# Attention and a Fourier mixing layer on one core: the mixing's chunk sums formed in two instalments, and the second weight matrix's combinations spread over 22 products instead of 28

## The chip, the cores and the metric

The kernel runs on one core of a Trainium2 chip. The metric is the device time of one execution in microseconds (us). A core has a matrix engine (PE, TensorE, with its weight loads shown apart as PEld), a vector engine (DVE, VectorE), a scalar engine (ACT, ScalarE), a general engine (POOL, GpSimd) and a queue that issues nearly all transfers (SP). [...]

## The reference

There are 8 batches. For each batch, 8 heads of attention with 576 positions and a head width of 64 give a matrix `x` of 576 by 512. A score counts only if it lies within `tau` of its row's maximum. Then `x` goes through a two-dimensional Fourier transform, whose real part is added to it, through a normalization and through two matrices with a ReLU between them:

```
scores = scale * q @ k.T;  thresh = max(scores) - tau
attn = softmax(where(scores >= thresh, scores, -1e9));  x = attn @ v      # 8 heads side by side: 576 x 512
X = fft(fft(x, axis=1), axis=2);  u = x + real(X)
un = (u - mean(u)) / sqrt(var(u) + 1e-6)
out = u + relu(un @ w_ch1) @ w_ch2          # w_ch1: 512 x 2048, w_ch2: 2048 x 512
```

## The kernel before, in words

**Attention steps.** Heads are handled in pairs, four pairs a batch, in the order 1, 3, 0, 2 of the four 128-wide chunks of `x` (`PAIRS`). A pair takes five steps of 128 query rows (the fifth takes the last 64 rows of both heads), so a batch is 20 steps and the whole is 160. A step `i` is called here by its place in its batch, `i % 20`. A step computes scores on PE (L440, L446), row maxima on DVE (L520), exponentials on ACT (L526), the threshold on DVE (L540), the division on ACT (L549); one step later PE transposes the weights through PSUM (L587, L605) and ACT copies them out (L593, L607). Every second step or so PE multiplies with `v` (L636).

**Mixing.** The Fourier transform uses the symmetries of sine and cosine. When a pair of heads is done, `fold_rows` adds and subtracts mirrored rows of its chunk of `x` and writes the chunk `f[:, p, :]`: an even half `E` of 304 columns and an odd half `O` of 304 columns. The first three pairs are folded by POOL (L687, L692, L699, L703), the last one by DVE, in step 1 of the next batch. After that the four chunks are combined with each other, which is what the change touches. With c0 to c3 for the chunks:

- `fold_halves`, on POOL, when chunks 1 and 3 are there: c1+c3 goes to the tile `sums`, c1-c3 replaces c3 (L718, L719, 608 columns each).
- `mixing`, on DVE, when the last chunk (2) is there: c0+c2 and c0-c2 (L718, L719, 608 columns each), then five sums and scaled sums of 304 columns (L744, L740 three times, L749). They stand in three pieces: two 608-column operations; `f0E` and `f1E`; then `f2E`, `f3O` and `f0O`.

PE then multiplies the results with cosine and sine tables (L759): first `py` of the even halves, which reads f0E, f1E and f2E in this order, later `py` of the odd halves, which reads f0O and f3O. ACT copies each `py` out of PSUM (L764, L769). PSUM tiles of this kind, also those of the transposes and of the matrix products, share four buffers (tag `mm`).

The pieces of `mixing` are handed out by `mix(1)`. In the main loop (batches 2 to 7) the first piece stands on DVE behind the thresholds of step 2 (L540). The second comes later in the same step, after PE has transposed the first half of the weights of step 1. The third comes in step 3, behind that step's maxima on DVE (L520) and its exponentials on ACT (L526). The `py` products of PE stand after it.

**The two matrices.** The tokens of all batches form groups of 512 (`NG` = 9). Group 0 is computed plainly (`channels`); the others use a two-level scheme with seven products instead of eight at each level (`two_level`), in which combinations of weight blocks stand in place of the blocks. The combinations of both matrices are formed once, written to DRAM (`f1`, `f2`) and then read back for each group in transfers of 1 MB to three buffers in turn (L1067, `ensure`). `w2_forms` is the generator that forms those of the second matrix on DVE and POOL (L1002) and sends them to DRAM from SP (L1012, L1016, L1019, and L1028 for the combinations, which stand in `room`, the tile `w1[3]`). Its last 16 pieces are taken in `two_level` of group 1, at chosen ones of the seven products of each of the four parts (L1236). When all products of the first matrix are through, POOL forms `s1_tile` in four operations (L1149). `s1_tile` is the same memory as `room`. After it POOL forms combinations of the hidden layer (L1184) that PE needs for the second matrix's products (L1391).

**What sets the order.** Everything from L104 on stands in an order written by hand (`manual_schedule`). A budget in `fill` decides how many of the two matrices' products are put into each step: it counts matrix columns, not time. `fold_more` takes one piece of a pair's folding per call; it is called in steps with `t > 2` and from `background`.

## Time and profile before

| | |
|---|---|
| time, median of three executions | 1574.54 us (1570.67 to 1574.88) |
| time of the profiled execution | 1571.28 us |
| its span, first to last instruction | 1569.5 us |
| PE busy | 1530.0 us, 97% |
| DVE busy | 1059.4 us, 68% |
| ACT busy | 917.8 us, 58% |
| POOL busy | 774.2 us, 49% |
| mean share of the TensorE clock granted | 0.993 |

A group of the profile is one line of the kernel on one engine with its count, its busy time, the mean length of one, and the idle time of the engine just before such instructions with the instruction that ended it ("10.6 <-DVE f L740 8.8": 10.6 us idle in all, 8.8 of it ended by DVE at L740). In a timeline, the first column is the start, the second the length, and a bracket at the end is the idle time before it and its releaser. The matrix engine records two entries for each fp32 product. The records of PE are modelled at their ends, so a gap between two of them is the least that it stood still.

### The profile page before, as it was taken

The page shows a single profiled execution, that of the slowest core. Times are in us where ns is not written, and L with a number is a line of the kernel's source. Part 1 is how long each engine was busy: PE and PEld are TensorE (multiplying, and loading weights), DVE is VectorE, ACT ScalarE, POOL GpSimd, SP SyncE. Part 2 cuts the span into 40 slices and gives each one's busy share as a digit, 9 for nine tenths or more (in the row PEclk, how much of TensorE's full clock was granted, in tenths as well). Part 3 has the DMA queues.
Part 4 walks back from the last instruction along what each step waited for, and adds up shares of the span by engine and source line. Part 5 has one row for each costly group of instructions (what it writes and reads, how often), then busy time and mean ns, then how long its engine had stood idle before and what let it go on. Part 6 is the DMA issues. An engine that isn't in the chain of part 4 may idle for free.

```text
span 1569.5 us, 27006 instructions
## 1 busy us (share of the span) xinstructions
PE 1530.0 (97%) x9786; PEld 1190.0 (76%) x9786; DVE 1059.4 (68%) x2119; ACT 917.8 (58%) x1921; POOL 774.2 (49%) x962
## 2 busy tenths in 40 slices
PE   9999999999989999999999999999999999999999
PEld 4555555556778778877788878887787878889999
DVE  6987676746769466766577566856677666755546
ACT  6875675655646576656666666666666676232231
POOL 3774553034355643546254724554264625546735
PEclk9999999999999999999999999999999999999999
DMA  6423234366756354634464354635464434646655
GB/s 167 129 58 117 77 91 116 125 204 178 240 185 197 86 175 130 180 108 144 144 184 138 116 148 140 194 94 159 128 189 132 143 118 148 222 143 234 234 201 182
DMA packets 248907, 239.31 MB, mean 152 GB/s; under 512 B 197027, under 2 KB 218533, under 8 KB 228678
## 3 DMA queue, kind: packets, MB, share of 16 engines
q1 hardware_dynamic: 246262, 237.28, 49.3%
q8 instruction: 78, 1.28, 0.3%
q10 hardware_dynamic: 2512, 0.30, 0.1%
q14 instruction: 55, 0.45, 0.1%
HBM read 205.93 MB, written 31.46 MB: 151 GB/s over the span
## 4 chain that ended last, share of the span: by engine, by line
PE 83%; DVE 10%; ACT 3%; DMA 1%; POOL 1%; issue 1%; SPq 0%; DVEq 0%; ACTq 0%; POOLq 0%
PE ph L1203 24%; PE po L1391 17%; PE pv L636 9%; PE sc L440 9%; PE pw L605 7%; PE po L926 4%; PE ph L902 3%; PE sc L446 2%; PE py L759 2%; PE pe L587 1%; PE pa L776 1%; DVE neg L520 1%; PE pa L780 1%; PE po L1370 1%; PE pn L851 1%
## 5 line engine op out<-in xcount | busy, mean ns | idle before, releaser
L520 DVE TENSOR_REDUCE neg<-sc 128x1 f32<-128x576 f32 x216 | 154.2, 751 | 131.2 <-PE sc L440 113.8
L526 ACT ACTIVATE e<-sc,neg 128x576 f32<-128x576 f32 x216 | 158.6, 734 | 120.5 <-DVE neg L520 120.5
L1391 PE MATMUL po<-w,w_all 128*128 128x128 f32 x1728 | 222.2, 278 | 5.1 <-DMA w<-f 2.7
L1391 PEld LDWEIGHTS po<-w,w_all 128*128 128x128 f32 x1728 | 207.6, 194 | 14.6 <-issue 9.1
L1140 DVE TENSOR_TENSOR hs<-ph,hs 128x512 f32<-128x512 f32 (+1 forms) x128 | 105.3, 823 | 164.7 <-PE ph L1203 96.2
L1149 POOL TENSOR_TENSOR w<-hs 128x512 f32<-128x512 f32 x32 | 41.9, 1314 | 310.5 <-ACT hs L1145 231.7
L1203 PE MATMUL ph<-u_t,w 128*128 128x256 f32 x768 | 180.9, 382 | 0.5 <-DMA w<-f 0.5
L540 DVE SCALAR_TENSOR_TENSOR e<-sc,thr,e 128x576 f32<-128x576 f32 x216 | 168.3, 812 | 18.8 <-ACT thr L530 18.7
L607 ACT COPY e_t<-pw 128x512 f32<-128x512 f32 x256 | 148.5, 595 | 54.0 <-PE pw L605 52.5
L605 PE MATMUL pw<-ident,e 128*128 128x128 f32 x1152 | 170.4, 275 | 4.6 <-ACT ends L593 1.9
L440 PE MATMUL sc<-kT,qT 64*128 64x288 f32 x1024 | 167.3, 428 | 6.4 <-DVE e L477 5.8
L549 ACT ACTIVATE e<-e,den 128x576 f32<-128x576 f32 x216 | 157.4, 775 | 8.0 <-DVE den L388 7.3
L1203 PEld LDWEIGHTS ph<-u_t,w 128*128 128x128 f32 x768 | 140.9, 190 | 23.6 <-issue 5.3
L1203 PE MATMUL ph<-w_all,w 128*128 128x256 f32 x672 | 157.1, 382 | 1.1 <-DVE w_all L1125 1.0
L605 PEld LDWEIGHTS pw<-ident,e 128*128 128x128 f32 x1152 | 136.3, 142 | 20.5 <-issue 5.8
L1203 PEld LDWEIGHTS ph<-w_all,w 128*128 128x128 f32 x672 | 123.5, 190 | 23.9 <-issue 4.9
L1145 ACT ACTIVATE hs<-hs 128x512 f32<-128x512 f32 (+1 forms) x96 | 74.1, 772 | 114.0 <-DVE hs L1140 113.4
L440 PEld LDWEIGHTS sc<-kT,qT 64*128 64x128 f32 x1024 | 95.0, 186 | 55.5 <-issue 25.1
L1256 POOL TENSOR_TENSOR w_all<-w_all 128x128 f32<-128x128 f32 (+2 forms) x160 | 116.6, 745 | 30.2 <-DVE w_all L1411 22.4
L1391 PE MATMUL po<-w,hs 128*128 128x128 f32 x912 | 120.0, 278 | 0.0
L1391 PEld LDWEIGHTS po<-w,hs 128*128 128x128 f32 x912 | 109.9, 192 | 9.5 <-issue 8.0
L593 ACT COPY ends<-pe 128x128 f32<-128x128 f32 (+1 forms) x128 | 38.1, 297 | 61.8 <-PE pe L587 41.6
(224 smaller groups left out, 2940.3 us busy)
## 6 DMA issues: line engine op xcount, KB each, us to landing
w<-f SPq DMA_DIRECT2D x150, 1024.0 KB, 4.9
hs<-in_moe_w_ch_dram SPq DMA_DIRECT2D x23, 512.0 KB, 4.7
q_in<-in_q_dram SPq DMA_DIRECT2D x128, 72.0 KB, 4.2
out_dram<-u SPq DMA_DIRECT2D x36, 256.0 KB, 2.3
k_in<-in_k_dram SPq DMA_DIRECT2D x124, 72.0 KB, 2.4
v_in<-in_v_dram SPq DMA_DIRECT2D x64, 128.0 KB, 5.1
f<-w SPq DMA_DIRECT2D x14, 512.0 KB, 3.3
f<-w SPq DMA_DIRECT2D x7, 1024.0 KB, 4.8
```

Of the source, the lines that this page charges most:

```text
L440: nc.tensor.matmul(sc[j][:, c, 0:HALF], qT[hp, 128 * t : 128 * t + 128], kT[hp, k0 + HALF * c : k0 + HALF * (c + 1)], start=True, stop=True,)
L520: nc.vector.tensor_reduce(out=neg[:, j : j + 1], in_=sc[j][:, :, 0:HALF], axis=AXIS_XY, op=ALU.max, negate=True,)
L526: nc.scalar.activation(out=ej, in_=sc[j][:, :, 0:HALF], func=ACT.Exp, bias=neg[:, j : j + 1], scale=1.0)
L540: nc.vector.scalar_tensor_tensor(out=ej, in0=sc[j][:, :, 0:HALF], scalar=thr[:, j : j + 1], in1=ej, op0=ALU.is_ge, op1=ALU.mult, accum_out ...
L549: nc.scalar.activation(out=e[:, S * j : S * (j + 1)], in_=e[:, S * j : S * (j + 1)], func=ACT.Copy, scale=den[:, j : j + 1],)
L605: nc.tensor.transpose(pw[:, c, :], e[:, c0 : c0 + 128], ident[:, :])
L607: nc.scalar.copy(e_t[:, 4 * j : 4 * j + 4, qs], pw[:, :, :])
L636: nc.tensor.matmul(pv[64 * j : 64 * j + 64, 0:m], vt[:, 2 * c + j, :], e_t[:, 4 * j + c, 0:m] if c < 4 else ends[:, 0, 0:m], start=(c == 0 ...
L1140: nc.vector.tensor_tensor(out=to, in0=bank, in1=to if other is None else other, op=ALU.add)
L1203: nc.tensor.matmul(bank[:, 256 * q : 256 * q + 256].rearrange("p (two n) -> p two n", two=2), left[:, 256 * c + 128 * q : 256 * c + 128 * ...
L1256: return lambda: eng.tensor_tensor(out=to, in0=to, in1=other, op=ALU.add)
L1391: nc.tensor.matmul(to, lefts[m][j][:, s], right_[:, 128 * s : 128 * (s + 1)], start=jn in (0, 4) and s == 0, stop=s == 3, skip_group_check ...
```

## The change

The sums of the chunks are taken apart. What needs chunks 0, 1 and 3 alone is formed ahead, by a new function `partial_sums`, while the last pair of heads is still in attention; when the last chunk is there, five operations of 304 columns are left. The partial results are c0+c1+c3 (E), c0-(c1+c3) (O), a scaled c1+c3 plus c0 (E), and two scaled combinations of c1-c3 with c0 (E and O). In `mixing`, the first piece is then f0E, f1E and f2E, the second f0O, the third f3O.

Batch by batch: in batch 0 the first two partial sums are on POOL and the other three on DVE behind the maxima; in batch 1 all five are on DVE at the end of step 19; in batches 2 to 7 three are on DVE in step 19 and two in step 0 of the next batch. So that chunk 0 is folded by then, `fold_more` is called in step 17 as well. In the diff, the loop over `partial_sums(1)` is batch 1's. The last hunks are in the main loop: there the first `next(partials)` of step 19 stands behind the thresholds of that step, as does that of step 0; the second one of step 19 stands after the transposes of the first half of the weights, ahead of `fill`. One more `next(partials)` behind the loop serves the last batch.

The second part is one number: pieces of `w2_forms` are taken at five of the seven products of a part instead of four, so the sixteenth piece is taken at the 22nd product instead of the 28th.

```diff
     def fold_halves(b):
         sums[b] = sb.tile([128, 2, 2 * FW], FP32, tag="tmp", bufs=1, name="sums")
-        fold_chunks(nc.gpsimd, b, 1)
-
-    def fold_chunks(eng, b, c):
-        eng.tensor_tensor(out=sums[b][:, c, :], in0=f[:, c, :], in1=f[:, c + 2, :], op=ALU.add)
-        eng.tensor_tensor(
-            out=f[:, c + 2, :], in0=f[:, c, :], in1=f[:, c + 2, :], op=ALU.subtract
+        for out_, op in ((sums[b][:, 1, :], ALU.add), (f[:, 3, :], ALU.subtract)):
+            nc.gpsimd.tensor_tensor(out=out_, in0=f[:, 1, :], in1=f[:, 3, :], op=op)
+
+    E, O = slice(0, FW), slice(FW, 2 * FW)
+
+    def scaled(out_, in0, factor, in1):
+        nc.vector.scalar_tensor_tensor(
+            out=out_, in0=in0, scalar=factor, in1=in1, op0=ALU.mult, op1=ALU.add
         )
+
+    def partial_sums(b, eng=nc.vector):
+        s = sums[b]
+        eng.tensor_tensor(out=s[:, 0, E], in0=f[:, 0, E], in1=s[:, 1, E], op=ALU.add)
+        eng.tensor_tensor(out=s[:, 0, O], in0=f[:, 0, O], in1=s[:, 1, O], op=ALU.subtract)
+        yield
+        scaled(s[:, 1, E], s[:, 1, E], flip, f[:, 0, E])
+        yield
+        scaled(f[:, 3, E], f[:, 3, E], minus, f[:, 0, E])
+        scaled(f[:, 3, O], f[:, 0, O], plus, f[:, 3, O])
+        yield
...
-        fold_chunks(nc.vector, b, 0)
+        s = sums.pop(b)
+        for c in range(2):
+            nc.vector.tensor_tensor(out=f[:, c, E], in0=s[:, c, E], in1=f[:, 2, E], op=ALU.add)
+        nc.vector.tensor_tensor(out=f[:, 2, E], in0=f[:, 3, E], in1=f[:, 2, E], op=ALU.subtract)
         yield 0
-        s01 = sums.pop(b)
...
-        nc.vector.tensor_tensor(out=f[:, 0, E], in0=s01[:, 0, E], in1=s01[:, 1, E], op=ALU.add)
-        fold(f[:, 1, E], s01[:, 1, E], flip, s01[:, 0, E])
+        nc.vector.tensor_tensor(out=f[:, 0, O], in0=s[:, 0, O], in1=f[:, 2, O], op=ALU.add)
         yield 0
-        fold(f[:, 2, E], f[:, 3, E], minus, f[:, 2, E])
-        fold(f[:, 3, O], f[:, 2, O], plus, f[:, 3, O])
-        nc.vector.tensor_tensor(out=f[:, 0, O], in0=s01[:, 0, O], in1=s01[:, 1, O], op=ALU.subtract)
+        scaled(f[:, 3, O], f[:, 2, O], minus, f[:, 3, O])
         yield 0
...
-                if at in (0, 2, 4, 6):
+                if at in (0, 2, 3, 4, 6):
                     next(forms, None)
...
+        if first == 19:
+            for _ in partial_sums(1):
+                pass
...
+        if i % per_batch == 19:
+            partials = partial_sums(i // per_batch)
+            next(partials)
+        if i % per_batch == 0 and i > 2 * per_batch:
+            next(partials)
...
-        if t > 2:
+        if t > 2 or i % per_batch == 17:
             fold_more()
+        if i % per_batch == 19:
+            next(partials)
```

The order of instructions on PE and on ACT is the same in both programs. DVE has 18 rows of instructions more, POOL two (the first batch's two partial sums), and SP the same number in another order.

More of the change, by code (lines that the diff above doesn't have):

```diff
@@ L730, in mixing @@
         slot = slice(S * (b % 2), S * (b % 2) + S)
-        E, O = slice(0, FW), slice(FW, 2 * FW)
-        fold_chunks(nc.vector, b, 0)
+        s = sums.pop(b)
+        for c in range(2):
+            nc.vector.tensor_tensor(out=f[:, c, E], in0=s[:, c, E], in1=f[:, 2, E], op=ALU.add)
+        nc.vector.tensor_tensor(out=f[:, 2, E], in0=f[:, 3, E], in1=f[:, 2, E], op=ALU.subtract)
         yield 0
-        s01 = sums.pop(b)
-        def fold(out_, in0, factor, in1):
-            nc.vector.scalar_tensor_tensor(
-                out=out_, in0=in0, scalar=factor, in1=in1, op0=ALU.mult, op1=ALU.add
-            )
-        nc.vector.tensor_tensor(out=f[:, 0, E], in0=s01[:, 0, E], in1=s01[:, 1, E], op=ALU.add)
-        fold(f[:, 1, E], s01[:, 1, E], flip, s01[:, 0, E])
+        nc.vector.tensor_tensor(out=f[:, 0, O], in0=s[:, 0, O], in1=f[:, 2, O], op=ALU.add)
         yield 0
-        fold(f[:, 2, E], f[:, 3, E], minus, f[:, 2, E])
-        fold(f[:, 3, O], f[:, 2, O], plus, f[:, 3, O])
-        nc.vector.tensor_tensor(out=f[:, 0, O], in0=s01[:, 0, O], in1=s01[:, 1, O], op=ALU.subtract)
+        scaled(f[:, 3, O], f[:, 2, O], minus, f[:, 3, O])
         yield 0
@@ L1656, in second_batch @@
             scores(i)
+        partials = iter(())
         if first == 0:
+            partials = partial_sums(0, nc.gpsimd)
+            next(partials)
             transposed_weights(i - 1)
         def behind_maxima():
+            for _ in partials:
+                pass
             if first == 2:
@@ L1720, in second_batch @@
             fold_halves(1)
+        if first == 19:
+            for _ in partial_sums(1):
+                pass
         if first < 3:
@@ L1772 @@
         next(weights, None)
-        if t > 2:
+        if t > 2 or i % per_batch == 17:
             fold_more()
+        if i % per_batch == 19:
+            next(partials)
         fill()
@@ L1798 @@
         held.pop(0)()
+    next(partials)
     weights = weights_in_parts(total - 1)
```

## The prediction

> **What bounds the kernel now.** I read the page's busy shares and its chain first.

> ```profile
> PE 1530.0 (97%) x9786; PEld 1190.0 (76%) x9786; DVE 1059.4 (68%) x2119; ACT 917.8 (58%) x1921; POOL 774.2 (49%) x962
> ...
> PE 83%; DVE 10%; ACT 3%; DMA 1%; POOL 1%; issue 1%; SPq 0%; DVEq 0%; ACTq 0%; POOLq 0%
> ```

> PE sets the end. The change takes no product from PE, so it can win only PE's idle time, 35.8 us by my sum of the gaps between its records, and what products lose at half clock. The groups by line on PE show the gaps that it can touch:

> ```profile
> L1391 PE MATMUL po<-w,w_all 128*128 128x128 f32 x1728 | 222.2, 278 | 5.1 <-DMA w<-f 2.7 <-POOL w_all L1184 2.1 <-ACT ends L593 0.3
> ...
> L759 PE MATMUL py<-dim_c,f 128*128 128x65 f32 (+3 forms) x144 | 21.6, 280 | 10.6 <-DVE f L740 8.8 <-DVE w_all L1411 1.6
> ```

> The second line is the mixing, once a batch; the first one's 2.7 and 2.1 are two single waits in group 1. PE's timeline in batch 5, and then in group 1:

> ```profile
> 1018.32 0.56 PE L759 MATMUL py<-dim_c,f 128*128 128x65 f32 x4
> 1020.90 0.49 PE L759 MATMUL py<-dim_c,f 128*128 128x128 f32 x2 [2.02 <-DVE f L740]
> 1021.22 0.27 PE L587 MATMUL pe<-ident,e 128*128 128x128 f32 x1
> 1021.33 0.60 PE L605 MATMUL pw<-ident,e 128*128 128x128 f32 x4
> 1022.11 0.71 PE L759 MATMUL py<-dim_s,f 128*128 128x128 f32 x4 [0.18 <-ACT y_e L769]
> ```
> ```profile
> 449.55 0.60 PE L605 MATMUL pw<-ident,e 128*128 128x128 f32 x4
> 452.85 1.92 PE L1391 MATMUL po<-w,w_all 128*128 128x128 f32 x8 [2.70 <-DMA w<-f]
> ```

> In batch 5 two `py` products (f0E, f1E) run, and the third waits 2.02 us for f2E, which DVE forms only behind two maxima (1018.22 to 1019.63). The gaps of batches 2 to 7 at this place are 1.18, 1.51+0.70, 2.03, 2.02, 2.03 and 1.56; batch 0 has 0.47, batch 1 none. For group 1, POOL's and SP's timelines say what was late:

> ```profile
> 443.41 1.66 POOL L1002 TENSOR_TENSOR w<-w_all,w 128x512 f32<-128x512 f32 x1 [9.07 <-DVE w L1002]
> 450.27 5.38 POOL L1149 TENSOR_TENSOR w<-hs 128x512 f32<-128x512 f32 x4 [5.20 <-DMA f<-w]
> ```
> ```profile
> 445.10 0.33 SPq L1028 DMA_DIRECT2D f<-w  x1
> 445.52 1.32 SPq L1067 DMA_DIRECT2D w<-f  x2
> ```

> The last combination is formed at 443.41 to 445.07. L1028, which writes it out, blocks SP until 445.10; only then are the loads behind it issued, of which PE waits for one until 452.85. L1149, which overwrites `room`, waits until L1028 has landed, so L1184 ends late and PE waits again, 2.15 us at 456.92. Windows (stretch, length, busy us and count of PE, PEld, DVE, ACT, POOL, then granted clock, DMA share, GB/s):

> ```profile
> 452.90:459.70 6.80, 4.65 (x21) 4.36 (x22) 1.49 (x3) 0.00 (x0) 6.80 (x9) 0.51 0.83 287
> 848.90:852.30 3.40, 3.40 (x15) 3.01 (x15) 3.33 (x10) 1.96 (x5) 0.00 (x0) 0.51 0.41 164
> 1021.00:1024.40 3.40, 3.22 (x26) 2.63 (x27) 3.33 (x10) 2.52 (x7) 0.00 (x0) 1.00 0.41 164
> ```

> So the gaps of group 1, batch 4 and (at 1193.7) batch 6 are followed by half clock, that of batch 5 is not.

> [...]

> **The change part by part.**

> *Second matrix's combinations.* The sixteenth piece comes six products earlier. Group 1's 28 products fill 351 to 441 us, 3.2 each, so L1028 leaves at about 445.1-19 = 426. SP is then free when the loads' buffers are, about 430 at the latest estimate, for products at 449.55: 20 us against a landing of 7.2 us here (median 4.9). L1149 can then start at its relu, about 443.4, and end, at 1.31 each, just after 444.7 for the last; L1184 by about 446, ahead of 451.5, where PE would want it. Gone: 2.70+2.15, and the half clock: 21 records at a spacing of 0.213 instead of 0.111 lose 2.1. **-6.95.** Price: 16.3 us of DVE's work falls into 71 instead of 90 us, 23% for 18%, where DVE is 69% busy and PE already waits 1.85 in all on L1140's release of banks: **+0.5**, from 0 to +3.

> *Mixing, batches 2 to 7.* f2E is now in the first piece, three 304-column operations (1.42-1.47) in place of two of 608 (1.56), so the third `py` product follows the second. What is late next is ACT: the odd `py` needs the bank that ACT's y_e copies free, and these stand behind the exponentials (until 1020.62 in batch 5): 0.63+ later PE goes at about 1021.2 rather than 1022.11. So batch 5 gains 0.9 of 2.0. Likewise batch 2: 0.8; batch 3: 0.36; batch 4: 1.33, with 0.81 of half clock (3.46 instead of batch 5's 2.65 us from the odd `py` to the next scores); batch 6: 0.94+1.56 (4.21 instead of 2.65); batch 7: 1.56, since its wait was on L1411. **-8.3.** If the ACT copies hide as well, all 11.0 of gaps go. Batch 0, its f2E earlier: **-0.5.**

> *DVE's five partial sums.* Per batch DVE had 2x0.78+3x0.526+2x0.47 = 4.1 us; after it has 4.9: two of 0.474 and three of 0.526 ahead, four of 0.474 and one of 0.526 in `mixing`. What matters is that 1.5 us now stands in step 19 and 1.05 in step 0. Behind them on DVE are the maxima of steps 0 and 1, for which ACT's exponentials wait, and then PE's transposes. DVE is idle 0.9 and 0.6 us ahead of those maxima, and the transposes of step 1 stand 1.9 to 2.8 us behind ACT's division. Without POOL the shift is taken up. A POOL operation at the same time adds about 1.0 (1.43 less 0.47) to each: The trace of before can't show how often that happens here; I take one meeting that shows on PE, in one batch of the six: **+1.0**, from 0 to R2's value below. Batch 1 has all five in step 19, 2.5 us, against 2.6 of slack ahead of the scores and 4.0 ahead of the transposes: **+0.2**. With this cover gone each batch would pay its 2.5 us.

> *Moves.* Step 17's extra `fold_more` puts POOL's folds ahead of one or two L1184. Chunk 0 was folded at 799.90 in batch 4, and DVE wants it about 812.6: 12 us to spare, so **0**. Batch 0's two sums on POOL, an estimated 0.8 us each (its 608-column operations take 1.47), stand behind copies of tables where nothing of PE waits for POOL: 0. PE's and ACT's orders don't change. SP has the same transfers.

> Sum: -6.95+0.5-8.3-0.5+1.0+0.2 = **-14.05**. Profiled execution: 1571.28-14.05 = 1557.2. The median of the three lay 3.26 above it: forecast **1560.5 us**.

> **Rivals.**
> R1, half of it: either group 1's wait stays, because its loads run at 0.83 DMA share and land late whenever they go, or `py` waits for its bank and not for f2E, so that the mixing's change doesn't do what it says. For: the 7.2 us landing; ACT's 0.18 in batch 5. Against: the releasers are named DVE f L740 and L1028. Without group 1's part 1574.5-8.8+1.7 = 1567.4; without the mixing's 1574.5-6.95+1.7 = 1569.3. So **1568**.
> R2, slower: DVE's queue at the batch boundary. If all five partial sums meet POOL they take 2.5+5x1.0 = 7.5 us; less 1.5 of idle (0.9+0.6) the exponentials come 6.0 later, against 2.8 of slack: PE waits 3.2 us in six batches, 19.2, and each such wait can bring a half-clock window (half of 3.4: 1.7 us), 10.2. Against gains of 15.75 (6.95+8.3+0.5) that is +13.65: **1588**. Without the windows it decides where the shift passes 2.8+15.75/6 = 5.4 us. For: DVE's forms vary threefold, POOL folds chunk 0 about then. Against: the fold ends 12 us earlier and POOL is 49% busy.
> R3, all of it: full gaps 11.0, batch 0's 0.5, group 1's 4.85, half clock 2.1+2.4, and an estimated 1.6 as the small waits behind them go too, no penalty: -22: **1552**.
> R4, the denser combinations cost their +3: 1563, on the forecast's side.

> **How the numbers follow.** Forecast with R4: 0.60, own range 1555 to 1565; R1 0.20; R3 0.11; R2 0.09. What this measurement can tell from no change is about 0.3%, 4.7 us: 1569.8. Faster holds the forecast, R3, and 0.14 of R1: 0.85; within: 0.06 of R1 and 0.03 of R2's mild end: 0.09; slower 0.06. The 80% range leaves out half of R3 and most of R2 and a little of R1: **1552 to 1570**.

> **What would show it.** Right: L1391 loses its 2.7 and 2.1 and 453 to 460 is at full clock; L1028 issues near 426 and L1149's wait names ACT; L759's idle falls from 10.6 to about 4 and names ACT y_e. Wrong: L587 and L605 gain idle time behind DVE in steps 0 and 1 (R2); L759 keeps its sum under another name (R1); L1140 on DVE delays L1203 (R4); or half-clock windows come back at other gaps, which is what I can least exclude.

## The result and the profile after

The changed kernel takes 1551.36 us in the median of four executions (1549.43 to 1552.64), the kernel before beside it 1573.1 (1570.67 to 1574.88): a ratio of 0.9862, 95% interval 0.9841 to 0.9882. A second set of runs gave 1551.38 us and a ratio of 0.9858 (0.9843 to 0.9874). The forecast was 1560.5; the time lies 9.1 us below it and 0.6 us below the lower end of the 80% range. The direction was right, the size was not.

The profiled executions compare as 1571.28 before (span 1569.5) and 1552.55 after (span 1550.8). The page after, its busy shares and its chain:

```profile
PE 1523.1 (98%) x9786; PEld 1185.1 (76%) x9786; DVE 1066.9 (69%) x2141; ACT 917.1 (59%) x1921; POOL 776.8 (50%) x964
...
PE 84%; DVE 9%; ACT 3%; DMA 1%; POOL 1%; issue 1%; SPq 0%; ACTq 0%; DVEq 0%; POOLq 0%
```

PE has the same 9786 records of products, yet its busy time fell by 6.9 us (from 1530.0), and the gaps between its records fell from 35.8 to 24.1 us in all, 11.7. The two make 18.6 of the span's 18.7 us. Most of the fall in busy time is half clock: the trace of before has six windows of 3.41 us at a granted clock of 0.50 (at 16.09, 101.42, 453.00, 456.41, 848.94 and 1193.69 us), that of after has one (82.22), not counting the one in which each trace ends. At 0.50 the four records of the odd `py` cover 1.10 us (before, batch 4, 850.43), at 1.00 they cover 0.71 (batch 5, 1022.11). A part is not: where a gap breaks a row of products, their records overlap less (in batch 5 the six of the even `py` cover 0.56 and 0.49 us before and 0.83 us after, both at full clock). So this is only a first division of the gain: about two thirds gaps, the rest for the most part clock. DVE has 22 operations more in the profile (2141 to 2119), where the text above counts 18.

The groups on PE that answer to those shown of before:

```profile
L1398 PE MATMUL po<-w,w_all 128*128 128x128 f32 x1728 | 219.4, 276 | 0.3 <-ACT ends L593 0.3
...
L766 PE MATMUL py<-dim_c,f 128*128 128x65 f32 (+3 forms) x144 | 19.2, 269 | 0.1
...
L766 PE MATMUL py<-dim_s,f 128*128 128x128 f32 (+1 forms) x96 | 15.4, 283 | 2.4 <-ACT y_e L776 2.4
```

The 2.7 and 2.1 us of group 1 are gone, and the even `py` waits 0.1 us in all instead of 10.6. What is left of the mixing's wait is at the odd `py`, 2.4 us, and it names ACT's copy of y_e, as the prediction said that it would. PE's timeline in batch 5:

```profile
1004.25 2.05 PE L1398 MATMUL po<-w,hs 128*128 128x128 f32 x16
1006.14 0.83 PE L766 MATMUL py<-dim_c,f 128*128 128x65 f32 x6
1006.81 0.27 PE L587 MATMUL pe<-ident,e 128*128 128x128 f32 x1
1006.92 0.60 PE L605 MATMUL pw<-ident,e 128*128 128x128 f32 x4
1008.19 0.71 PE L766 MATMUL py<-dim_s,f 128*128 128x128 f32 x4 [0.67 <-ACT y_e L776]
```

The odd `py` starts 2.05 us behind the first even one; it was 3.79 (1018.32 to 1022.11). Group 1 on SP and on POOL:

```profile
425.20 0.34 SPq L1035 DMA_DIRECT2D f<-w  x1
425.63 15.42 SPq L1074 DMA_DIRECT2D w<-f  x3
```
```profile
430.89 3.73 POOL L1156 TENSOR_TENSOR w<-hs 128x512 f32<-128x512 f32 x3
442.94 1.72 POOL L1156 TENSOR_TENSOR w<-hs 128x512 f32<-128x512 f32 x1 [8.32 <-ACT hs L1152]
```

The last combinations leave at 425.20 (L1028 before, L1035 now), three of POOL's four operations are done by 434.6, and the fourth waits for ACT's relu and no longer for a transfer.

Where the 18.7 us went is read from the starts of the scores of the 160 steps, one trace less the other. Around group 1 the changed kernel gains 7.5 us; around the mixings of batches 2 to 7 it gains 1.4, 1.3, 2.95, 1.75, 3.3 and 1.8, together 12.5; in batches 0 and 1 it gains 0.5 in all (single steps there move by up to 1.7 us either way, mostly with windows of half clock); and it loses 1.1 at the start of batch 5 and some 0.65 in other places.

### The profile page after: what moved, and what is told of

It is laid out like the page before. It is cut to its first block, busy times and chain, and to the rows that moved or that the text cites. A ratio compares the mean times of both kernels' runs of the same rounds, so it can differ in the third digit from the quotient of the medians.

```text
span 1550.8 us, 27036 instructions
## 1 busy us (share of the span) xinstructions
PE 1523.1 (98%) x9786; PEld 1185.1 (76%) x9786; DVE 1066.9 (69%) x2141; ACT 917.1 (59%) x1921; POOL 776.8 (50%) x964
## 3 DMA queue, kind: packets, MB, share of 16 engines
q8 instruction: 78, 1.28, 0.3%
## 4 chain that ended last, share of the span: by engine, by line
PE 84%; DVE 9%; ACT 3%; DMA 1%; POOL 1%; issue 1%; SPq 0%; ACTq 0%; DVEq 0%; POOLq 0%
PE ph L1210 25%; PE po L1398 18%; PE sc L440 9%; PE pv L636 9%; PE pw L605 7%; PE po L933 4%; PE ph L909 2%; PE sc L446 2%; PE py L766 2%; PE pa L783 1%; PE pe L587 1%; PE pa L787 1%; PE pm L360 1%; PE po L1377 1%; PE pn L858 1%
## 5 line engine op out<-in xcount | busy, mean ns | idle before, releaser
L605 PE MATMUL pw<-ident,e 128*128 128x128 f32 x1152 | 168.8, 273 | 6.0 <-ACT ends L593 1.9
L605 PEld LDWEIGHTS pw<-ident,e 128*128 128x128 f32 x1152 | 134.8, 141 | 21.9 <-issue 5.6
L593 ACT COPY ends<-pe 128x128 f32<-128x128 f32 (+1 forms) x128 | 38.1, 298 | 58.7 <-PE pe L587 40.1
```

Of the source, the lines that this page charges most:

```text
L605: nc.tensor.transpose(pw[:, c, :], e[:, c0 : c0 + 128], ident[:, :])
```

## The experiments

Two theories stood against each other on the mixing. A: ahead of the maxima of step 3 DVE works off an unbroken row, and the change made that row shorter, so maxima, exponentials and y_e all come earlier. B, a step of the forecast: the maxima stay where they were, and only f2E's place behind them counted.

**Each part alone.** The combinations of the second matrix alone, on the kernel before:

```diff
-                if at in (0, 2, 4, 6):
+                if at in (0, 2, 3, 4, 6):
```

> The kernel before with the second matrix's combinations alone made denser (sixteenth piece at the 22nd product). Theory A, waits of group 1: the two waits of 2.70 and 2.15 us and the half clock behind them go, as between the two traces (7.5 us from step 58 to step 59): 7.5 us below before, about 1565.6, no new wait at DVE's additions of the hidden layer, and the waits of py stay at 9 to 10 us. Rival, crowding: the loads land late whenever they go out and the wait only moves; then within 3 us of before.

Measured: 1562.21 us, 0.9937 of before (0.9916 to 0.9957), which is 6.8 to 13.2 us of the 1573.28 beside it. In the trace the gain around group 1 is 7.5 us, and the waits of `py` are those of before:

```profile
L1391 PE MATMUL po<-w,w_all 128*128 128x128 f32 x1728 | 220.4, 277 | 0.3 <-ACT ends L593 0.3
...
L759 PE MATMUL py<-dim_c,f 128*128 128x65 f32 (+3 forms) x144 | 22.5, 290 | 10.6 <-DVE f L740 8.8 <-DVE w_all L1411 1.6
```

The rival, that the loads land late whenever they go out, falls. The waits for L1140's additions add up to 1.8 us in 351 to 441, as before, so the half microsecond that I charged for a denser DVE was not paid.

How much earlier is enough? The sixteenth piece at the 26th product:

```diff
-                if at in (0, 2, 4, 6):
+                if at in (0, 2, 4, 6) or (part == 3 and at == 3):
```

> As the last, but the sixteenth piece at the 26th product, some 6 us earlier than before instead of 19. If the two waits of group 1 have separate causes (a load queued on SP behind the write of the last combination; POOL, which may overwrite the same memory only when that write has landed), they part here: the write leaves at about 439, the load's wait of 2.70 us is gone or under 0.5, while POOL's four operations can start only at about 443.5, end at 449, and PE still waits 1 to 2.5 us for POOL; 3 to 6 us below before. If one cause makes both, both go (7.5 us below before) or both stay.

Measured: 1563.97 us, 0.9938 (0.9914 to 0.9961), and again 7.45 us around group 1. My expectation that the two waits part was wrong: both are gone. POOL's timeline shows that its wait is still there, and PE's that no wait comes of it:

```profile
444.85 5.52 POOL L1149 TENSOR_TENSOR w<-hs 128x512 f32<-128x512 f32 x4 [5.10 <-DMA f<-w]
450.31 1.28 POOL L1184 TENSOR_TENSOR w_all<-hs 128x512 f32<-128x512 f32 x1
451.54 1.28 POOL L1184 TENSOR_TENSOR w_all<-hs,w_all 128x512 f32<-128x512 f32 x1
```
```profile
450.77 2.03 PE L1391 MATMUL po<-w,w_all 128*128 128x128 f32 x16
452.64 0.60 PE L605 MATMUL pw<-ident,e 128*128 128x128 f32 x4
453.08 1.06 PE L1391 MATMUL po<-w,w_all 128*128 128x128 f32 x8
```

The 16 records at 450.77 are two products. The second begins at 451.68; it is the one that waited until 456.92 before, and it begins 0.09 us behind the end of POOL's first sum (450.31 + 1.28). The next product, at 453.08, begins 0.26 us behind the end of the second (452.82). POOL is thus just in time, with no room to spare. I had expected PE to want these sums 1 to 2.5 us before they are there; the 451.5 of the prediction was nearer. Some 5 us of lead (the write leaves at 439.77 instead of 445.10) bought what 20 us buys: 7.45 us around group 1 here and 7.5 there.

The mixing alone, on the changed kernel:

```diff
-                if at in (0, 2, 3, 4, 6):
+                if at in (0, 2, 4, 6):
```

> The changed kernel with the combinations at their old pace: only the mixing's sums are changed. Theory A, that DVE's row of work ahead of the maxima of step 3 became 0.67 us shorter, so that maxima, exponentials and the copies of y_e come earlier: 12 us below before, about 1561, with the odd py starting 2.05 us behind the first even one in batches 4 to 6 as in the changed kernel, and group 1 keeping its 2.7 and 2.1 us. Theory B, the step of the forecast (maxima stay where they were): 7.6 us below before, and the rest of the gain belongs to the two parts together.

Measured: 1558.83 us, 0.991 (0.9889 to 0.9931), 14 us below before with an interval from 11 to 17. In the trace the odd `py` starts 2.04 to 2.05 us behind the even one in batches 4 to 6, and group 1 keeps 2.6 and 2.6 us. Theory A's 12 lies in the interval and B's 7.6 does not. The gains of the two parts, 9.9 and 14.2 by their ratios, make 24 with errors of 3 each: they add up to the 21.7 to 22.3 of both within these.

**What in the mixing did it.** The kernel before, with f2E alone taken from behind the maxima to ahead of them, and no sum formed in advance:

```diff
         fold(f[:, 1, E], s01[:, 1, E], flip, s01[:, 0, E])
-        yield 0
         fold(f[:, 2, E], f[:, 3, E], minus, f[:, 2, E])
+        yield 0
         fold(f[:, 3, O], f[:, 2, O], plus, f[:, 3, O])
```

> The kernel before with f2E moved from behind the maxima to ahead of them, and no sum formed in advance. py no longer waits behind the maxima in either theory. Theory A: the maxima and all behind them come 0.53 us later, so the odd py starts as late as before or 0.2 us earlier, and the gap only changes its name to ACT y_e: 0 to 2 us below before for the gaps, up to 4 with the half clock of two batches. Theory B: the place of f2E is what counted and the forecast's 0.9 us a batch is gained here too: 6 to 8 us below before.

Measured: 1571.41 us, 0.9989 (0.998 to 0.9998), a gain of 1.7 us (0.3 to 3.1). Theory B's 6 to 8 us are out. The groups on PE:

```profile
L759 PE MATMUL py<-dim_c,f 128*128 128x65 f32 (+3 forms) x144 | 20.0, 273 | 2.5 <-DVE w_all L1411 2.0
L759 PE MATMUL py<-dim_s,f 128*128 128x128 f32 (+1 forms) x96 | 15.7, 287 | 8.2 <-DVE f L749 8.1 <-ACT y_e L769 0.2
```

The even `py` lost its wait for L740 and the odd one took it over, 8.2 instead of 1.1 us, for f0O (L749) and not, as I had written, for y_e: DVE has as much to do between the thresholds and the odd sums as ever. Here moving one operation to the other side of the maxima moved the wait and did not remove it.

The change's row was then lengthened and shortened by one operation. Lengthened, with f3O ahead of the maxima:

```diff
         nc.vector.tensor_tensor(out=f[:, 0, O], in0=s[:, 0, O], in1=f[:, 2, O], op=ALU.add)
-        yield 0
         scaled(f[:, 3, O], f[:, 2, O], minus, f[:, 3, O])
         yield 0
+        yield 0
```

> The changed kernel with f3O moved from behind the maxima of step 3 to ahead of them, the reverse of what the change did to that row. Theory A, the row of DVE's work ahead of the maxima sets when the odd py can start: maxima, exponentials and y_e come 0.53 us later in batches 2 to 6, the wait of the odd py for ACT y_e grows from 0.67 to 1.2 us in batches 4 to 6 and the sum over five batches is 2.6 us: 2 to 4 us above the changed kernel. Rival, that only ACT's own queue or DVE's work behind the maxima sets it: within 0.5 us of the changed kernel.

Shortened, with f0O behind them:

```diff
-        nc.vector.tensor_tensor(out=f[:, 0, O], in0=s[:, 0, O], in1=f[:, 2, O], op=ALU.add)
         yield 0
+        nc.vector.tensor_tensor(out=f[:, 0, O], in0=s[:, 0, O], in1=f[:, 2, O], op=ALU.add)
         scaled(f[:, 3, O], f[:, 2, O], minus, f[:, 3, O])
```

> The changed kernel with f0O moved from ahead of the maxima to behind them. Theory A alone: maxima 0.47 us earlier in batches 2 to 6, wait for ACT y_e from 0.67 down to 0.2, 2 us below the changed kernel. Theory A with POOL in the way: both f0O and f3O now stand where POOL's 2.09 us operation shuts out DVE (f3O alone takes 1.31 there instead of 0.53), so the odd py waits for DVE instead, as late as now or up to 0.3 us later a batch: within 1.5 us of the changed kernel, with the wait named DVE L721 or L754.

Measured: 1553.34 us (0.9896, 0.9882 to 0.9909) and 1550.9 us (0.9877, 0.9864 to 0.9891). The changed kernel itself did not run beside these two, nor beside the next two; they are compared with it by their medians, and the traces have to bear the argument. By the ratios to the kernel before, which took 1570.33 us beside them, each of the four lies some 3 us higher. PE's timeline in batch 5, f3O ahead and then f0O behind:

```profile
1005.22 0.83 PE L766 MATMUL py<-dim_c,f 128*128 128x65 f32 x6
...
1007.72 0.71 PE L766 MATMUL py<-dim_s,f 128*128 128x128 f32 x4 [1.12 <-ACT y_e L776]
```
```profile
1004.21 0.83 PE L766 MATMUL py<-dim_c,f 128*128 128x65 f32 x6
...
1005.87 0.71 PE L766 MATMUL py<-dim_s,f 128*128 128x128 f32 x4 [0.29 <-ACT y_e L776]
```

Counted from the first even `py` of batch 5:

| kernel | maxima start | exponentials end | odd py starts |
|---|---|---|---|
| before | -0.10 | +2.30 | +3.79 |
| f3O ahead | -0.47 | +1.93 | +2.50 |
| changed | -0.92 | +1.48 | +2.05 |
| f0O behind | -1.30 | +1.09 | +1.66 |

The last three rows move together, 0.4 us for each operation: the chain from DVE's row over maxima, exponentials and y_e to PE is shown. In the kernel before, the odd `py` stands later than this chain alone would put it, since y_e there also waits for the third even product and so for f2E. With f3O ahead, the time is 2.0 us above the changed kernel, the lower end of the 2 to 4 expected, and the steps of its trace lose 0.3 to 0.45 us in each of five batches, 2.1 in all. With f0O behind, f0O was drawn out to 1.31 us instead of 0.47 (as f3O is beside POOL in the changed kernel, 1.31 instead of 0.53), but it was done at 1005.55, ahead of the odd `py`, and PE still named ACT. So f0O's new place ahead of the maxima is not what made the gain. The gap of 0.39 us that each batch saves comes back in part as 0.27 us at the next even `py`, which waits for ACT's y_o, so the time hardly moves: expected was 2 us below the changed kernel or none, and a difference of 0.5 us is within the scatter.

**What the five sums cost.** The changed kernel with the first two partial sums formed three times:

```diff
-        eng.tensor_tensor(out=s[:, 0, E], in0=f[:, 0, E], in1=s[:, 1, E], op=ALU.add)
-        eng.tensor_tensor(out=s[:, 0, O], in0=f[:, 0, O], in1=s[:, 1, O], op=ALU.subtract)
+        for _ in range(3 if b > 1 else 1):
+            eng.tensor_tensor(out=s[:, 0, E], in0=f[:, 0, E], in1=s[:, 1, E], op=ALU.add)
+            eng.tensor_tensor(out=s[:, 0, O], in0=f[:, 0, O], in1=s[:, 1, O], op=ALU.subtract)
```

> The changed kernel with the first two partial sums formed three times over in step 19 of batches 2 to 7 (the same values): 4 x 0.46 = 1.85 us more on DVE at each batch boundary. If the slack behind it is what the trace of before showed (transposes of step 0 stand 3.0 us behind the division, and the scores of the next step 2.2 to 2.5 us behind the thresholds), only batch 5's start, where PE already waits 1.52 us for ACT's copy of a product, pays the 1.85: 2 to 4 us above the changed kernel with its half clock. Rival R2 of the forecast, each boundary pays: 1.85 us in six batches, 11 us or more above.

Measured: 1563.38 us (0.9956, 0.9943 to 0.9968), 12 us above the changed kernel: the rival R2, which I had put at 11 or more, and not the 2 to 4 that I read from the slack. The spans of the two profiled executions lie 8.8 us apart and the ratios give 15; both are far from 2 to 4. The starts of the steps give 1.0, 2.1, 4.1, 2.1 and 1.8 us at five boundaries, part of it taken back in batches 0 and 1, which the edit leaves alone. DVE and PE at the start of batch 5:

```profile
804.23 0.47 DVE L731 TENSOR_TENSOR sums<-f,sums 128x304 f32<-128x304 f32 x1
804.61 1.54 DVE L730 TENSOR_TENSOR sums<-f,sums 128x304 f32<-128x304 f32 x1
...
809.02 1.42 DVE L520 TENSOR_REDUCE neg<-sc 128x1 f32<-128x576 f32 x2
```
```profile
807.67 0.27 PE L587 MATMUL pe<-ident,e 128*128 128x128 f32 x1
811.93 1.12 PE L605 MATMUL pw<-ident,e 128*128 128x128 f32 x4 [3.98 <-ACT w_all L1411]
```

One sum meets a POOL operation (804.33 to 805.82) and takes 1.54 instead of 0.47 us, the maxima start at 809.02, and PE waits 3.98 us for an ACT copy behind their exponentials. The granted clock of this execution was 0.998, that of the changed kernel's profiled one 0.999. At three other boundaries PE waits 1.23 us for ACT's copy of `x` (L643). The slack that I had used, of scores and of transposes, left out these copies, which stand on ACT behind the exponentials of step 0 and free the banks of PE. So 1.9 us more of DVE's work at each boundary eats about half of the change's gain.

The same two sums on POOL:

```diff
-            partials = partial_sums(i // per_batch)
+            partials = partial_sums(i // per_batch, nc.gpsimd)
```

> The changed kernel with the first two partial sums of batches 2 to 7 on POOL instead of DVE. In step 19 DVE then has 0.94 us less ahead of its own additions for the hidden layer. If the meeting of these with a POOL addition (1.57 instead of 0.69 us) is what makes PE wait 1.52 us at the start of batch 5, that wait falls to about 0.4 to 0.6 and nothing else moves: 1 us below the changed kernel. Rival: POOL's own row is now 1.6 us longer and its additions, or DVE shut out by them, come later: 0 to 3 us above.

Measured: 1549.83 us (0.9867, 0.9851 to 0.9882). The one wait that the change brought, at the start of batch 5, falls from 1.52 to 1.02 us:

```profile
807.60 0.66 PE L605 MATMUL pw<-ident,e 128*128 128x128 f32 x4 [1.02 <-ACT w_all L1410]
```

That is half of what I expected (0.4 to 0.6 was to be left), and PE still names ACT's copy. The time is below the changed kernel's by 1.5 us, but their executions overlap.

**The changed kernel again, and both moves in it** (f0O behind the maxima, two sums on POOL):

> The changed kernel as it is, for a comparison on the same chip as the next one. With few half-clock windows left its executions should lie within 4 us of each other, near 1551, and the kernel before should spread over 6 to 10 us with the granted clock of each execution.

> The changed kernel with f0O behind the maxima and the first two partial sums of batches 2 to 7 on POOL. From the two single runs' traces: 0.5 us at the start of batch 5 and 0.1 us net in each of five batches, so 1 us below the changed kernel; the rival, that the two stand in each other's way on POOL and DVE, gives 0 to 1 us above it.

Measured: 1551.38 us (0.9858, 0.9843 to 0.9874) and 1550.54 us (0.9851, 0.9838 to 0.9865). The 0.8 us between them can't be told from none. No version here beats the changed kernel by more than the measurement can tell.

The repetition did show what the executions of one kernel differ by. The eight of the changed kernel, both sets together, lie between 1549.43 and 1553.63. Those of the kernel before lie between 1567.96 and 1577.89 over 43 executions, and the granted clock of each execution goes with its time (correlation -0.95): 1568.4 us in the mean at 0.997, 1575.9 at 0.991. A straight line through them, drawn out to full clock, meets it at 1564.5, some 8 us below their median of 1572.85. As an estimate from this line, about so much of the time before was half clock.

## Why the prediction was wrong in size

**What bounds the kernel, and group 1.** Right. The write of the last combinations was late, both waits came of it, and both went. It was put at -6.95 and +0.5 and measured -7.5: L1028 at 425.2 where 426 was forecast, the cost of the denser DVE not paid. The other 0.55 us was not taken apart.

**Mixing, batches 2 to 7.** Put at -8.3, measured -12.5. Here is the first step that failed: "these stand behind the exponentials (until 1020.62 in batch 5)". The next limit was named rightly, ACT's y_e, but I left the exponentials where they were. They follow the maxima, and the maxima follow a row of DVE's work that had no idle time in batches 4 to 6. DVE in batch 5, before and after:

```profile
1015.10 0.79 DVE L719 TENSOR_TENSOR f<-f 128x608 f32<-128x608 f32 x1
1015.92 0.47 DVE L744 TENSOR_TENSOR f<-sums 128x304 f32<-128x304 f32 x1
1016.31 0.53 DVE L740 SCALAR_TENSOR_TENSOR f<-sums,factors 128x304 f32<-128x304 f32 x1
1016.76 0.68 DVE L1411 TENSOR_TENSOR w_all<-w_all,po 128x512 f32<-128x512 f32 x1
...
1018.22 1.41 DVE L520 TENSOR_REDUCE neg<-sc 128x1 f32<-128x576 f32 x2
```
```profile
1002.98 0.48 DVE L752 TENSOR_TENSOR f<-f 128x304 f32<-128x304 f32 x1
1003.38 0.47 DVE L754 TENSOR_TENSOR f<-sums,f 128x304 f32<-128x304 f32 x1
1003.76 0.68 DVE L1418 TENSOR_TENSOR w_all<-w_all,po 128x512 f32<-128x512 f32 x1
...
1005.22 1.42 DVE L520 TENSOR_REDUCE neg<-sc 128x1 f32<-128x576 f32 x2
```

The mixing's operations in this row begin 4.04 us ahead of the first even `py` in both kernels (1014.28 and 1002.10). From there to L1411, now L1418, took 2.48 us and takes 1.66, so maxima, exponentials and y_e came 0.82 us earlier against PE. I had compared the first pieces alone (1.42 to 1.47 us in place of 1.56), and not the second, which went from two operations (f0E, f1E) to one (f0O). By the starts of the steps the gain was missed by 0.8 us in each of batches 4 to 6, which is this 0.82. In batches 2 and 3, where the maxima came 0.57 and 0.64 us earlier, it was missed by 0.6 and 0.9, in batch 7 by 0.2: together 4.2. Batch 0, put at -0.5, gains 1.4 at its mixing; that batches 0 and 1 come to just 0.5 in all is luck, since windows of half clock and two losses of 0.5 and 0.7 us in batch 1 stand against it. The trace of before shows this row without a gap; the forecast left that out.

**Half clock.** In the mixings it was priced rightly: from the odd `py` to the next scores batches 4 and 6 now take the 2.65 us of batch 5, which is the 0.81 and 1.56 that I had charged. The second step that failed is "The median of the three lay 3.26 above it": I priced half clock from one execution, and carried this difference over to the changed kernel as if it were noise. The times of the 43 executions go with their granted clocks (the -0.95 above), so such differences are for the most part half clock. The traces show where it falls: that of before has it behind the mixings of batches 4 and 6 (0.50 from 848.94 and from 1193.69) and not behind that of batch 3 (1.00 from 678.28), that of the denser combinations alone, with the same mixing, has it behind that of batch 3 (0.50 from 669.9), and this execution took 1567.29 us at a granted clock of 0.994 where the other four of its kernel took 1561.93 to 1563.93 at 0.997 and 0.998. After the change the median lies 1.2 us below its profiled execution, so this step alone is 4.5 of the 9.1 us; the mixing's 4.2 and group 1's 1.05 are the rest, less 0.55 that the other losses were larger than I put them.

**DVE's partial sums.** +1.0 was put down for one meeting with POOL that shows on PE, in one batch. The size was right, 1.1, and so was the count of one batch, but it is not a sum that meets POOL. At the start of batch 5 the sums push DVE's L1191, an addition of the hidden layer, against POOL's L1191 (803.45 to 805.22); it takes 1.57 instead of 0.69 us, and PE's wait for ACT grows from 0.41 to 1.52:

```profile
804.19 1.57 DVE L1191 TENSOR_TENSOR w_all<-w_all,hs 128x512 f32<-128x512 f32 x1
```
```profile
808.58 0.66 PE L605 MATMUL pw<-ident,e 128*128 128x128 f32 x4 [1.52 <-ACT w_all L1410]
```

R2 named the mechanism rightly, with the wrong margin: it was to decide where the shift passes 5.4 us, and the tripled sums, a shift of 3.3 us in step 19 before POOL's share, already cost 12. The slack of 2.8 us in that sum was too large.

**The rivals.** R3's time (1552) came about, but not as R3 had it: 3.5 of the 11.8 us of gaps around the mixings are left, and between the medians half clock gave more than was allowed it. R1 and R4 are out: neither half of the change failed, and L1140's waits stayed.

## What to carry to other kernels

When work is moved or removed on an engine that feeds a chain, ask first whether the row ahead of the chain's head has any idle time in it. Here it had none in batches 4 to 6, and all that stood behind the head moved with the row's length, the next limit as well: 0.4 us for each operation. In this kernel moving one operation to the other side of the head only renamed the wait (8.8 us for L740, then 8.1 for L749), and shortening the row took most of it away (2.4 us left). And where the executions of a kernel differ by several microseconds, read the granted clock of each one before taking the difference for noise: the gaps that a change closes may be what makes them differ. Last, work put into a gap has to be held against every consumer behind it: here the slack was read from two, and a third, ACT's copies, set the cost (with the sums tripled, PE waited 3.98 us for them at the start of batch 5).

## What the runs showed of the hardware

About half a window of idle PE was enough here for half clock in the next one. From 150 us on and counting windows at full clock, in the trace of before those with 1.68, 2.03 and 2.70 us of idle PE were followed by one at 0.50, and the six with 1.06 to 1.56 us by one at 1.00; in that of the changed kernel the two with 1.08 and 1.52 us were followed by one at 1.00; in that of the denser combinations alone one with 1.80 us (666.45 to 669.85) was followed by one at 0.50. In the first 150 us, where PE runs other products, windows with 1.08 and 1.09 us of gaps were followed by half clock in the kernel before, one with 1.06 us was not, and neither was one with 1.03 us in the changed kernel, and I don't know why.

So the same gap of 2 us cost 2.0 us in batch 5 and 3.2 in batch 4, by where it fell: against batch 5, half clock added 1.2 us in batch 4 (0.39 up to the odd `py` and 0.81 behind it) and 1.56 in batch 6. Four windows of the kernel before (stretch, length, then busy us and count of PE, PEld, DVE, ACT, POOL, granted clock, DMA share, GB/s), cut at the clock's own bounds:

```profile
845.50:848.90 3.40, 1.37 (x14) 1.23 (x12) 3.40 (x6) 1.56 (x3) 2.08 (x1) 1.00 0.70 222
848.95:852.30 3.35, 3.35 (x15) 2.96 (x15) 3.28 (x10) 1.96 (x5) 0.00 (x0) 0.50 0.40 161
1016.20:1019.60 3.40, 2.68 (x24) 2.31 (x20) 3.40 (x8) 0.91 (x2) 1.16 (x1) 1.00 0.31 60
1019.65:1023.00 3.35, 1.93 (x15) 1.69 (x15) 3.35 (x7) 2.35 (x8) 0.86 (x1) 1.00 0.80 328
```

Batch 4's gap of 2.03 us lies whole in the first window, PE is busy 1.37 of 3.40 us, and the next window runs at 0.50. Batch 5's gap of 2.02 us is cut by the bound at 1019.6; its two windows have 2.68 and 1.93 us of busy PE, and the clock stays. This was the open point of the prediction ("that of batch 5 is not"). In the trace of the changed kernel no window from 150 us on has more than 1.52 us of idle PE until PE's last products are done, and none of these is followed by half clock.

The price of 1.0 us that the forecast put on a meeting of DVE with POOL is read from L744, an addition of 304 columns on DVE. In the trace of before it took 1.43 us in the one of its eight executions that lay beside a POOL operation, and 0.46 to 0.48 us in the other seven. It ended 0.33 us behind that operation (671.75 and 671.42). The six of L740 that took 1.29 to 1.54 us instead of 0.52 to 0.53 also ended 0.33 us behind a POOL operation; five additions of 608 columns (L718, L719) that took 1.74 to 1.87 us instead of 0.77 to 0.79 ended 0.65 us behind one. In the changed kernel f3O in batch 5 did the same: 1.31 us instead of 0.53, its end 0.33 us behind POOL's L1344 (1005.45 to 1007.54).
